# A top-32 attention with a metaformer block on one core: the next unit's halves are formed ahead of a unit's last maximum

## The chip, the cores and the metric

The kernel runs on one core of a Trainium2 chip. A core has five engines, each with a queue that is worked off in order: TensorE (PE in the profile; its weight loads are PEld), VectorE (DVE), ScalarE (ACT), GpSimd (POOL) and SyncE (SP, which here issues nearly all DMAs). Engines wait for each other by semaphores. The metric is the time of one execution on the device in microseconds; lower is better.

## The reference

For 8 batches, 8 heads, 576 rows and 64 columns a head, each row of scaled scores is cut to its 32 largest, softmax is taken over these, and the result is multiplied with the values. The heads are joined to rows of 512, and a layer norm, two matrix products with a ReLU between (512 to 2048 and back) and a residual follow.

```python
scores = scale * np.matmul(q, k.transpose(0, 1, 3, 2))
kth = np.partition(scores, -top_k, axis=-1)[..., -top_k:-top_k + 1]
scores = np.where(scores >= kth, scores, -1000000000.0)
scores = scores - np.max(scores, axis=-1, keepdims=True)
attn = np.exp(scores)
attn = attn / (np.sum(attn, axis=-1, keepdims=True) + 1e-09)
x = np.matmul(attn, v)            # heads joined to rows of 512
xn = (x - mu) / np.sqrt(var + 1e-06) * g_ln
out = x + np.maximum(xn @ w_ch1, 0.0) @ w_ch2
```

## The kernel before, in words

**Units.** A unit is 128 query rows of two heads, two tiles of 128 x 576 scores, or, for the 64 rows that 576 leaves over, one tile that holds these rows of both heads. There are 160 units, 128 of two tiles and 32 of one. A loop over n (in `compute`) takes one unit after the other, and in each round every engine gets work of several units: TensorE makes the scores of unit n + 2 (`scores`, line 438), VectorE selects in unit n, ScalarE and GpSimd mask unit n - 1, and the exponentials of unit n - 1 and n - 2 are turned and multiplied with the values.

**Selection on VectorE.** `halve` (line 447) forms the elementwise larger and smaller halves of a score row: line 461 writes 288 larger values to `hi`, line 462 the smaller to `lo`. `hi` has two homes, taken in turn by units, `lo` one. `select(u, i)` (line 464) finds eight maxima at a time (line 483) and strikes them out (line 469), for i from 0 to 3, so 32 in all; at i = 1 the eight largest of `lo` are added to the candidates (line 475). At i = 3 nothing is struck out: its eighth maximum is the unit's threshold `thr`.

**From the threshold on.** In the next round `prepare` lets ScalarE scale the threshold and the top (lines 495 and 496); `mask` makes a steep ReLU on ScalarE (line 532) and subtracts the scores on GpSimd (line 535). `watch` (line 502) notes on GpSimd whether a row had more than eight of its 32 among the smaller halves. `weigh` takes the exponential on ScalarE (line 543).

**Turning.** Attention weights are transposed in one of two ways: by TensorE (`turn`, line 606, evacuated by ScalarE, line 618), or, for most later units, "moved": VectorE transposes blocks of 32 (`move`, line 577), and two DMAs of SyncE carry them by way of memory into `pt` (lines 594 and 587). `values` (lines 669 and 677) multiplies them, ScalarE evacuates to `oT` (line 687), TensorE turns that (line 714), and ScalarE scales it into rows (line 691).

**Row work.** Finished rows get statistics on VectorE (`stats`, lines 742 and 743) and are centred on GpSimd (lines 748 and 751); TensorE turns them (line 778), ScalarE evacuates (line 781), and the products of lines 819 and 979 follow, whose ReLU (line 842) and sums are on ScalarE and GpSimd. In the first rounds the weights are converted too (lines 164 to 185, on ScalarE, GpSimd and, line 177, VectorE).

**Order.** The schedule is written out by hand (`manual_schedule`): instructions stand in each queue as the program issues them. Only the matrix products of the row work are placed by a planner: `fill` issues as many of them as a share per slot allows, from costs that are constants in the source. PSUM has 5 banks for short-lived tiles (scores, turned tiles, values) and 3 for the row work's products. Score tiles in SBUF have 5 buffers.

Of the kernel before, what the change touches and what calls it, by code (L numbers as in the profile page):

```python
# [29 lines left out]
def compute(  # L30
# [207 lines left out]
    def pop():  # L238
        kind, cost, run, may = todo.pop(0)
        assert not may or may()  # L240
        owed[0] -= cost
        run()
# [30 lines left out]
    def fill(least=0):  # L273
        tick[0] += 1
        loads.settle(LOAD_AGE)
        sends.settle(SEND_AGE)
        ends_later.settle(END_AGE)
        fetch_forms(FETCH_AGE)
        owed[0] = min(owed[0] + share[0], 6.0)
        while todo and (not todo[0][3] or todo[0][3]()):  # L280
            if owed[0] < todo[0][1] / 2 and least <= 0:
                break
            least -= 1
            pop()
# [162 lines left out]
    def halve(u):  # L447

        nt = len(u.tiles)
        u.lo = lopool.tile([P, 2, HALF], FP32, tag="lo", name="lo")
        u.hi = hi_homes[u.i % 2]
        sides = int(doubt is not None)
        u.low, u.body = (sides * LOWS + HALF, sides * LOWS) if doubt is None or u.i // 2 % 2 else (0, LOWS)
        a, b = u.sc[:, 0:nt, 0:HALF], u.sc[:, 0:nt, HALF:S]
        lo, hi = u.lo[:, 0:nt], u.hi[:, 0:nt, u.body : u.body + HALF]  # L460
        nc.vector.tensor_tensor(hi, a, b, ALU.max)  # L461
        nc.vector.tensor_tensor(lo, a, b, ALU.min)  # L462

    def select(u, i):

        nt = range(len(u.tiles))

        def replace(m, t, x):
            nc.vector.match_replace(x, m[:, t, :], x, LOWEST)  # L469

        if i == 1:
            for r in range(low_rounds):
                o = u.low + 8 * r
                for t in nt:
                    nc.vector.max(u.hi[:, t, o : o + 8], u.lo[:, t])  # L475
                if r < low_rounds - 1:
                    for t in nt:
                        replace(u.hi[:, :, o : o + 8], t, u.lo[:, t])
        r0, width = (min(u.low, u.body), HALF + LOWS) if i > 1 else (u.body, HALF)
        pl = brief_small if i in (1, 2) else small  # L480
        m = pl.tile([P, 2, 8], FP32, tag=f"m{i}", name=f"m{i}")
        for t in nt:
            nc.vector.max(m[:, t, :], u.hi[:, t, r0 : r0 + width])  # L483
        if i < TOP_K // 8 - 1:
            for t in nt:
                replace(m, t, u.hi[:, t, r0 : r0 + width])
        if i == 0:
            u.top = m
        u.thr = m
# [47 lines left out]
    def weigh(u, t):  # L537
        g = u.group
        if g.den is None:
            g.den = denpool.tile([P, 2 * J + 1], FP32, tag="den", name="den")  # L540
        col = 2 * u.qt + t
        u.weighed += 1
        nc.scalar.activation(  # L543
            u.e[:, t], u.e[:, t], AF.Exp, bias=u.bias[:, t : t + 1], scale=-scale,
            accum_out=g.den[:, col : col + 1],
        )
        if u.rest:
            den = g.den[:, 2 * J : 2 * J + 1]
        elif u.weighed == 2 and u is [x for x in g.units if not x.rest][-1]:
            whole = [qt for qt in g.qts if qt < J]  # L550
            den = g.den[:, 2 * whole[0] : 2 * whole[-1] + 2]
            g.sums = den
        else:
            return
        nc.scalar.activation(den, den, AF.Copy, bias=DEN_EPS)
# [500 lines left out]
    def fetch_forms(age):  # L1056
        if done(formed[0]):
            free = 4 + sum(tick[0] - x >= age for x in used)
            while fetched[0] < min(free, 8 * (len(blocks) - PLAIN)):
                fetch_form()  # L1060
# [96 lines left out]
    def at(i):  # L1157
        return units[i] if 0 <= i < N else None
# [104 lines left out]
    for n in range(END):  # L1263
# [8 lines left out]
        u, nxt, mk = at(n), at(n + 1), at(n - 1)  # L1272
# [119 lines left out]
        if mk and len(mk.tiles) > 1 and mk.i >= EARLY:  # L1392
            weigh(mk, 1)
        fill()
        if u:
            select(u, 3)
        if nxt:
            halve(nxt)
        if n == 0:
            for x in batches[-1]:  # L1400
                x.shift()
# [27 lines left out]
@with_exitstack  # L1429
def kernel(  # L1430
    ctx: ExitStack,
    tc: tile.TileContext,
    *operands: bass.AP,
):
    nc = tc.nc
    doubt = ctx.enter_context(tc.tile_pool(name="doubt", bufs=1)).tile(
        [1, 1], I32, tag="doubt", name="doubt"
    )
    compute(tc, *operands, low_rounds=1, doubt=doubt[:])
    again = nc.values_load(  # L1440
        doubt[:], min_val=0, max_val=1,
        skip_runtime_bounds_check_because="a comparison's result",
    )
    with tc.If(again > 0):
        compute(tc, *operands, low_rounds=2, doubt=None)
# [31 lines left out]
```

## Time and profile before

| | before |
|---|---|
| median of 3 runs (lowest to highest) | 1571.86 us (1570.28 to 1573.63) |
| the profiled execution's own time | 1571.11 us |
| its span | 1569.2 us |
| busy: TensorE, VectorE | 1469.0 us (94%), 1363.4 us (87%) |
| busy: ScalarE, GpSimd | 1083.8 us (69%), 981.2 us (63%) |

A span runs from the first to the last instruction of the program in the profile. A group of instructions is shown by its line, engine and operation, what it writes and reads, its count, its busy time and mean, and the idle time of its engine just before it with what ended that. A row of the timeline has start, duration, engine, line and operation, and in brackets the idle time before it and what released it. A row of waits has the total in us, the number of waits and the longest. TensorE's instruction ends are modelled, so its busy share tells that it has work, not that it is at its peak.

### The profile page before, as it was taken

How to read it: one execution, taken by the hardware profiler on the slowest of the kernel's cores; microseconds unless marked ns; L12 is line 12 of the kernel's file. 1: busy time of each engine (PE TensorE's matmuls, PEld its weight loads, DVE VectorE, ACT ScalarE, POOL GpSimd, SP SyncE). 2: the span in 40 equal slices, each digit the busy share in tenths (PEclk: the TensorE clock that was granted, in tenths of full speed). 3: DMA queues.
4: the chain of work that ended last, by engine and by line, in shares of the span. 5: the costliest groups of instructions: out<-in, count | busy, mean ns of one | idle time of the engine just before them, and what ended most of it. 6: DMA issues, size and time to landing. Idle time of an engine off the chain costs nothing. (4 is left out here: it accounts for less than half of the span.)

```text
span 1569.2 us, 27215 instructions
## 1 busy us (share of the span) xinstructions
PE 1469.0 (94%) x8046; PEld 1108.0 (71%) x8046; DVE 1363.4 (87%) x3873; ACT 1083.8 (69%) x3081; POOL 981.2 (63%) x1318
## 2 busy tenths in 40 slices
PE   4568889999999999999999999999999998999997
PEld 3346446566787677778777777777777776788886
DVE  7997999899979998999988999999999999768000
ACT  6978887786777767767768676768676776555421
POOL 6968995747465565756566647474746475737524
PEclk9779989999999999999999999999999999999999
DMA  6623551466728865577754687657677557454511
GB/s 170 167 85 97 137 139 53 124 178 181 226 83 194 202 208 153 168 199 153 216 148 134 174 200 197 173 150 191 175 201 206 162 164 208 121 166 125 150 35 50
DMA packets 374774, 245.60 MB, mean 157 GB/s; under 512 B 255956, under 2 KB 343512, under 8 KB 374616
## 3 DMA queue, kind: packets, MB, share of 16 engines
q1 hardware_dynamic: 371048, 243.17, 57.6%
q8 instruction: 67, 1.10, 0.3%
q10 hardware_dynamic: 3568, 0.59, 0.3%
q14 instruction: 91, 0.75, 0.2%
HBM read 166.14 MB, written 77.53 MB: 155 GB/s over the span
## 5 line engine op out<-in xcount | busy, mean ns | idle before, releaser
L535 POOL TENSOR_TENSOR e<-e,sc 128x576 f32<-128x576 f32 x288 | 416.0, 1462 | 453.8 <-ACT e L532 392.9
L819 PE MATMUL hps<-xT,w 128*128 128x256 f32 x2304 | 542.2, 384 | 2.4 <-ACT xT L781 2.4
L819 PEld LDWEIGHTS hps<-xT,w 128*128 128x128 f32 x2304 | 423.0, 191 | 82.2 <-issue 27.2
L483 DVE MAX8 m<-hi 128x8 f32<-128x296 f32 (+1 forms) x1152 | 471.3, 444 | 1.2
L469 DVE MATCH_REPLACE8 hi<-m,hi 128x288 f32<-128x288 f32 (+1 forms) x864 | 377.0, 441 | 0.0
L979 PE MATMUL ops<-w,h 128*128 128x256 f32 x1280 | 304.8, 383 | 1.4 <-ACT o L944 1.4
L979 PEld LDWEIGHTS ops<-w,h 128*128 128x128 f32 x1280 | 233.6, 190 | 44.3 <-issue 13.5
L419 ACT COPY sc<-scps 128x288 f32<-128x288 f32 x576 | 188.5, 402 | 78.5 <-POOL e L535 56.2
L543 ACT ACTIVATE e<-e,m 128x576 f32<-128x576 f32 x288 | 225.1, 784 | 14.6 <-POOL e L535 12.5
L532 ACT ACTIVATE e<-sc,m 128x576 f32<-128x576 f32 x288 | 209.4, 769 | 0.0
L842 ACT ACTIVATE h<-hps 128x512 f32<-128x512 f32 x144 | 86.7, 602 | 114.1 <-PE hps L819 113.5
L577 DVE STREAM_TRANSPOSE sc<-e 128x1152 f32<-128x1152 f32 x87 | 118.8, 1366 | 52.5 <-ACT e L543 46.3
L669 PE MATMUL av<-pt,vb 128*64 128x256 f32 (+2 forms) x1280 | 148.8, 376 | 9.5 <-DMA pt<-turned 7.7
L462 DVE TENSOR_TENSOR lo<-sc 128x576 f32<-128x576 f32 (+1 forms) x160 | 136.1, 850 | 0.0
L461 DVE TENSOR_TENSOR hi<-sc 128x576 f32<-128x576 f32 (+1 forms) x160 | 130.0, 812 | 3.0 <-ACT sc L419 3.0
L669 PEld LDWEIGHTS av<-pt,vb 128*64 128x64 f32 x1280 | 81.6, 140 | 66.4 <-issue 17.1
L438 PE MATMUL scps<-kT,late_qT 64*128 64x288 f32 (+3 forms) x832 | 121.7, 410 | 0.2 <-ACT pt L618 0.2
L979 PE MATMUL ops<-wt,s 128*128 128x256 f32 x512 | 119.4, 383 | 0.0
L475 DVE MAX8 hi<-lo 128x8 f32<-128x288 f32 x288 | 117.5, 443 | 0.0
L438 PE MATMUL scps<-kT,qT 64*128 64x288 f32 x512 | 92.6, 460 | 23.5 <-DVE qT L366 8.0
L606 PE MATMUL tp<-ident,e 128*128 128x128 f32 x456 | 74.2, 290 | 39.9 <-ACT e L543 28.9
L979 PEld LDWEIGHTS ops<-wt,s 128*128 128x128 f32 x512 | 94.7, 190 | 17.3 <-issue 4.4
(111 smaller groups left out, 1793.5 us busy)
## 6 DMA issues: line engine op xcount, KB each, us to landing
turned<-sc SPq DMA_DIRECT2D x87, 576.0 KB, 4.2
pt<-turned SPq DMA_DIRECT2D x348, 144.0 KB, 3.2
w<-forms SPq DMA_DIRECT2D x128, 256.0 KB, 4.7
vb<-in_v_dram SPq DMA_DIRECT2D x80, 288.0 KB, 4.2
raw<-in_moe_w_ch_dram SPq DMA_DIRECT2D x32, 512.0 KB, 4.5
kT<-kept SPq DMA_DIRECT2D x48, 288.0 KB, 3.7
kept<-kT SPq DMA_DIRECT2D x32, 288.0 KB, 3.6
kqin<-in_k_dram SPq DMA_DIRECT2D x116, 72.0 KB, 2.6
```

Source lines behind the costliest of these rows:

```text
L419: nc.scalar.copy(u.sc[:, t, s * HALF : (s + 1) * HALF], u.made[s][t][:, 0:HALF])
L438: nc.tensor.matmul(ps[i * R : i * R + ql, o : o + width], qT[r, q0 : q0 + ql], kT[r, k0 : k0 + width], start=True, stop=True,)
L461: nc.vector.tensor_tensor(hi, a, b, ALU.max)
L462: nc.vector.tensor_tensor(lo, a, b, ALU.min)
L469: nc.vector.match_replace(x, m[:, t, :], x, LOWEST)
L483: nc.vector.max(m[:, t, :], u.hi[:, t, r0 : r0 + width])
L532: nc.scalar.activation(u.e[:, t], u.sc[:, t], AF.Relu, bias=u.edge[:, t : t + 1], scale=-STEEP)
L535: nc.gpsimd.tensor_tensor(u.e[:, t], u.e[:, t], u.sc[:, t], ALU.subtract)
L543: nc.scalar.activation(u.e[:, t], u.e[:, t], AF.Exp, bias=u.bias[:, t : t + 1], scale=-scale, accum_out=g.den[:, col : col + 1],)
L669: nc.tensor.matmul(av[h * D : (h + 1) * D, 0 : g.nq], vb[:, h * (J + 1) + c, :], heads_of(g, h, 0, g.nq // 32)[:, :, c], start=(c == 0), s ...
L819: nc.tensor.matmul(ps[0][:, side * N : (side + 1) * N], w1[:, c, f * P : (f + 1) * P], self.xT[:, c, 0:N], start=(c == 0), stop=(c == NC - 1),
L979: nc.tensor.matmul(bank[name][:, 0:Q], a(j), rhs, start=first and j == 0, stop=(j == G - 1), skip_group_check=not first,)
```

## The change

In each round the halves of the next unit are formed ahead of `select(u, 3)`, the last maxima of the present unit, instead of behind it. For a unit of two tiles VectorE's queue held, at the end of a round: two replacements of i = 2 (line 469), two maxima (line 483), one operation of line 461 and one of line 462. It now holds the two replacements, lines 461 and 462, and then the two maxima. What stands in the other engines' queues, and what each instruction waits for, is the same as before.

```diff
@@ -1392,10 +1392,10 @@
         if mk and len(mk.tiles) > 1 and mk.i >= EARLY:
             weigh(mk, 1)
         fill()
+        if nxt:
+            halve(nxt)
         if u:
             select(u, 3)
-        if nxt:
-            halve(nxt)
         if n == 0:
             for x in batches[-1]:
                 x.shift()
```

## The prediction

> **What bounds the kernel now.** I read the page's busy times, then busy time by stage, then the waits of ScalarE and TensorE stage by stage, and last the timeline of single units. One execution was profiled at 1571.11 us (span 1569.2 us and 1.9 us around it); the median of the three runs is 0.75 us higher.
>
> ```profile
> span 1569.2 us, 27215 instructions
> ...
> PE 1469.0 (94%) x8046; PEld 1108.0 (71%) x8046; DVE 1363.4 (87%) x3873; ACT 1083.8 (69%) x3081; POOL 981.2 (63%) x1318
> ```
>
> Busy time by stage (stretch, its length, then PE, PEld, DVE, ACT, POOL):
>
> ```profile
> 0.00:220.00 220.00, 154.48 (x721) 99.86 (x722) 194.51 (x524) 182.17 (x469) 178.90 (x171) 0.87 0.51 134
> ...
> 310.00:416.00 106.00, 102.89 (x554) 73.74 (x553) 105.79 (x312) 75.55 (x215) 62.44 (x85) 0.98 0.70 186
> ...
> 475.00:590.00 115.00, 109.02 (x607) 83.61 (x605) 114.86 (x333) 78.67 (x227) 66.20 (x93) 0.99 0.78 203
> ...
> 862.00:1316.00 454.00, 445.25 (x2430) 335.21 (x2428) 451.73 (x1303) 325.34 (x956) 276.15 (x411) 1.00 0.68 181
> 1316.00:1460.00 144.00, 143.21 (x739) 117.32 (x740) 104.89 (x284) 77.13 (x211) 84.53 (x122) 1.00 0.55 154
> ```
>
> TensorE is the bound of the whole: after 220 us it is idle for a few us per stage, and its instructions do not change, so the time moves only as its idle time moves. But the pacemaker alternates. In 310 to 416, 475 to 590 and 862 to 1316 VectorE is busy for over 99% and TensorE loses 3.1, 6.0 and 8.75 us; from 1316 on TensorE paces and VectorE has spare time.
>
> The threshold (the last maximum of a unit, line 483) reaches ScalarE at line 495. That wait over the whole run, and then in 220 to 310, 310 to 416, 475 to 590, 740 to 789 and 862 to 1316:
>
> ```profile
> ACT m L495 <- DVE m L483: 84.2, 51, 3.7
> ...
> ACT m L495 <- DVE m L483: 2.9, 1, 2.9
> ...
> ACT m L495 <- DVE m L483: 17.2, 8, 3.5
> ...
> ACT m L495 <- DVE m L483: 21.4, 10, 3.7
> ...
> ACT m L495 <- DVE m L483: 4.8, 4, 2.2
> ...
> ACT m L495 <- DVE m L483: 37.9, 28, 3.4
> ```
>
> The five stretches hold all 51 waits and 84.2 us. Elsewhere, in the first 220 us too, ScalarE comes later than the threshold. What TensorE waited for (stretch 220 to 310, then 310 to 416, 475 to 590, and from 1316 on):
>
> ```profile
> PE scps L438 <- ACT x L691: 2.4, 1, 2.4
> ...
> PE av L669 <- DMA pt<-turned: 2.3, 1, 2.3
> PE xo L714 <- ACT oT L687: 0.8, 1, 0.8
> ...
> PE tp L606 <- ACT sc L419: 1.6, 1, 1.6
> ...
> PE tp L778 <- ACT sc L419: 1.9, 1, 1.9
> ```
>
> So where VectorE paces, TensorE meets ScalarE's copies, which stand behind the wait for the threshold.
>
> **The change, part by part.** No instruction is added or removed; the two halvings of the next unit (lines 461 and 462) go in front of the last maxima. The other queues, SP's and POOL's too, keep their order and no DMA is moved. A plain unit of two tiles now, in the timeline:
>
> ```profile
> 1183.56 0.74 DVE L461 TENSOR_TENSOR hi<-sc 128x576 f32<-128x576 f32 x1
> 1183.68 0.21 ACT L495 ACTIVATE m<-m 128x2 f32<-128x2 f32 x1 [0.58 <-DVE m L483]
> ...
> 1184.21 0.75 DVE L462 TENSOR_TENSOR lo<-sc 128x576 f32<-128x576 f32 x1
> 1184.77 2.84 POOL L535 TENSOR_TENSOR e<-e,sc 128x576 f32<-128x576 f32 x2 [1.83 <-ACT e L532]
> 1184.88 0.81 DVE L483 MAX8 m<-hi 128x8 f32<-128x288 f32 x2
> ```
>
> (1) *The threshold's delay.* From the first halving to the next maximum is 1184.88 - 1183.56 = 1.32 us; that is how much later each threshold comes (about half where the next unit has one tile). Queued on ScalarE behind line 495 are line 496, the masks of line 532, the copies of line 419 and then everything that frees PSUM or feeds TensorE; POOL's subtraction waits for the masks. VectorE gains nothing by having the halves earlier: it reads them itself, one maximum later.
>
> (2) *Units with row statistics.* These put two statistics on VectorE and two centrings on POOL (line 751) just ahead of the last maxima:
>
> ```profile
> 955.79 0.69 POOL L751 TENSOR_SCALAR x<-x,less 128x512 f32<-128x512 f32 x1
> ...
> 956.13 0.81 DVE L483 MAX8 m<-hi 128x8 f32<-128x296 f32 x2
> ...
> 956.74 1.32 POOL L751 TENSOR_SCALAR x<-x,less 128x512 f32<-128x512 f32 x1
> 956.85 0.74 DVE L461 TENSOR_TENSOR hi<-sc 128x576 f32<-128x576 f32 x1
> ...
> 957.50 1.16 DVE L462 TENSOR_TENSOR lo<-sc 128x576 f32<-128x576 f32 x1
> ...
> 958.55 1.27 ACT L419 COPY sc<-scps 128x288 f32<-128x288 f32 x4
> ...
> 958.98 0.66 PE L606 MATMUL tp<-ident,e 128*128 128x128 f32 x4 [1.40 <-ACT sc L419]
> ```
>
> A halving and a POOL operation exclude each other here: the second centring takes 1.32 instead of 0.69 us while line 461 runs, and line 462 then 1.16 instead of 0.75. After the change line 461 would start at 956.13, still under the first centring (to 956.48, 0.35 us lost), and the second centring would still come between the halvings (some 0.6 us). That is 0.95 us of collision instead of 0.41, so about 0.5 us more VectorE time in each such unit, and a threshold late by 1.32 + 0.95 = 2.3 us. The Trainium skill (SBUF — State Buffer, Who interferes with whom) says that a VectorE instruction with two SBUF inputs and a GpSimd instruction that reads SBUF lock each other out for a whole instruction, whoever issues first. By that rule the collision moves rather than vanishes; the trace agrees, with 1.16 against 0.75 us.
>
> (3) *Units of one tile.* Their last maximum directly follows the replacement that it reads, and VectorE pauses; with two tiles another instruction lies between:
>
> ```profile
> 793.04 0.45 DVE L469 MATCH_REPLACE8 hi<-m,hi 128x296 f32<-128x296 f32 x1
> ...
> 793.52 0.47 DVE L483 MAX8 m<-hi 128x8 f32<-128x296 f32 x1
> ...
> 782.24 0.44 DVE L469 MATCH_REPLACE8 hi<-m,hi 128x296 f32<-128x296 f32 x1
> 782.60 0.82 DVE L483 MAX8 m<-hi 128x8 f32<-128x296 f32 x2
> ```
>
> 0.48 against 0.36 us from start to start: the halvings would fill that pause, 0.12 us for each of these units, 14 of which lie in 862 to 1316 (the count of the one-tile form, quoted below), 1.7 us. The Trainium skill (VectorE: DVE Perf Modes, The DRAIN you can't avoid) says that an operation's pipeline flush is paid whether or not a semaphore follows. Read strictly, this saving would be nothing and a sum that counts it 1.7 us higher; these rows speak for a saving.
>
> (4) *VectorE's own balance.* Some six statistics units lie in VectorE-paced stretches beside the two counted below: 6 x 0.5 = +3 us against -1.7 us. I take 0 and keep both ends for the range.
>
> (5) *What reaches TensorE.* Where VectorE paces, a constant delay does not add up from unit to unit: ScalarE and TensorE run 1.3 us later against VectorE, once. But when the stretch ends and TensorE paces, it starts that much later, and nothing there gives it back. So each stretch is charged once, by what TensorE met last in it. 220 to 310: a wait for ScalarE, 1.3 us. 310 to 416: the wait for ScalarE is followed by one of 2.3 us for a DMA whose source VectorE sends at an unchanged place, which swallows the first delay; after it only slack, so half, 0.7 us. 475 to 590: the last wait, 1.6 us, is in a statistics unit, 2.3 us. 740 to 789: no wait within, half, 0.7 us. 862 to 1316: the wait of 1.9 us at its end is behind a statistics unit again, 2.3 us. Sum: 1.3 + 0.7 + 2.3 + 0.7 + 2.3 = 7.3 us, which only a gain in (4) could cancel. In the first 220 us ScalarE is late by itself and hides the delay; if that cover went, 1.3 us more.
>
> 1571.1 + 7.3 = 1578.4 us; I predict 1578, 0.4% above the median.
>
> **The rivals.** *The delay is swallowed.* Against 51 late thresholds TensorE has some 20 short waits after 220 us, and DMA waits that do not move take up part of it. If only one of the two statistics ends reaches it, 1571.1 + 2.3 = 1573.4 us: no difference that can be told, since 0.2% (3.1 us) is about what a measurement of this kernel can tell from no change.
>
> *Faster, by fewer collisions.* The halvings now follow the threshold, and so run while ScalarE's masks wake POOL's subtraction; moved forward they might miss POOL. VectorE's groups in 862 to 1316 by form (count, busy us and mean ns, idle before):
>
> ```profile
> L577 DVE STREAM_TRANSPOSE sc<-e 128x1152 f32<-128x1152 f32 x38 | 51.9, 1365 | 0.0
> ...
> L462 DVE TENSOR_TENSOR lo<-sc 128x576 f32<-128x576 f32 x42 | 34.6, 825 | 0.0
> L461 DVE TENSOR_TENSOR hi<-sc 128x576 f32<-128x576 f32 x42 | 32.5, 775 | 0.0
> ...
> L462 DVE TENSOR_TENSOR lo<-sc 128x288 f32<-128x288 f32 x14 | 7.4, 526 | 0.0
> ```
>
> Against the undisturbed 0.74 and 0.75 us the 42 pairs of two tiles lose 42 x (0.035 + 0.075) = 4.6 us, and against 0.45 us the 14 of one tile 14 x 0.076 = 1.1: 5.7 us are collisions. If all went, with the 1.7 us of (3), VectorE would save 7.4 us there, less than TensorE's idle 8.75: 1571.1 - 7.4 = 1563.7 us, and 1571.0 with the handed-over 7.3. It decides from about 10 us saved, so it needs the first 220 us as well. Against it: in the plain unit the halvings are already undisturbed (0.74, 0.75).
>
> *Much slower, by the moved units.* VectorE's transposes (line 577) wait for the exponential, whose chain starts at the threshold. A tight place:
>
> ```profile
> 1070.95 0.19 ACT L543 ACTIVATION_READ_ACCUMULATOR e<-e,m 128x1 f32 x1
> ...
> 1073.11 1.37 DVE L577 STREAM_TRANSPOSE sc<-e 128x1152 f32<-128x1152 f32 x1
> ```
>
> The spare time is 1073.11 - 1071.14 = 1.97 us, over 1.32 but under 2.3. From 1.97 us on VectorE, the pacemaker, stalls. If TensorE's lateness doubles the delay (2.64 us), each such move costs up to 0.67 us; ten of them give 1578.4 + 6.7 = 1585 us.
>
> **How the numbers follow.** The forecast case, 1575 to 1582, 0.45; the moved units 0.13; swallowed 0.22; fewer collisions 0.20. So slower 0.58, same 0.22, faster 0.20. Low is 1567, between the two prices of the faster rival; high is 1588, the 1585 of the moved units with the +3 us of (4).
>
> **What would show it.** Right: line 495's wait on the threshold grows from 84 us in 51 waits to some 150 us, by about 1.3 us each; TensorE's waits for lines 419 and 687 grow by some 7 us in total and its other numbers stay; VectorE's pause in units of one tile is gone; line 751 stays long. Wrong: halvings with a clearly lower mean, VectorE's busy time down by 10 us or more, or line 577 waiting in 862 to 1316, where it now waits for nothing (0.0 in its row above).

## The result, and the profile after

The changed kernel takes 1584.05 us (median of 6 runs, 1583.22 to 1585.78), the kernel before on the same chip 1571.18 us (6 runs, 1569.75 to 1573.63). The ratio is 1.0082 (95% interval 1.0069 to 1.0095): 12.9 us slower. The forecast was 1578 us; the sign and the kind of loss came out, and the loss is nearly twice the 7.3 us that were forecast.

The page of the changed kernel (span, then busy time of the engines):

```profile
span 1582.5 us, 27215 instructions
...
PE 1469.8 (93%) x8046; PEld 1107.9 (70%) x8046; DVE 1372.3 (87%) x3873; ACT 1083.9 (68%) x3081; POOL 993.9 (63%) x1318
```

TensorE has as much work as before (1469.8 against 1469.0 us), so the loss is idle time of TensorE. VectorE is busy for 8.9 us more and GpSimd for 12.7, with the same instructions: they hold each other up more.

The waits of the changed kernel over the whole run (who waits for whom: total in us, number, longest):

```profile
ACT m L495 <- DVE m L483: 126.2, 67, 5.4
...
DVE sc L577 <- ACT e L543: 48.0, 12, 8.8
...
PE tp L606 <- ACT sc L419: 23.1, 14, 3.2
...
PE xo L714 <- ACT oT L687: 7.8, 10, 1.3
...
PE tp L778 <- ACT sc L419: 6.2, 2, 5.5
...
PE av L669 <- DMA pt<-turned: 3.2, 3, 1.7
```

Two of these rows in the kernel before:

```profile
PE tp L606 <- ACT sc L419: 10.9, 7, 2.1
...
PE av L669 <- DMA pt<-turned: 7.7, 6, 2.9
```

ScalarE waits for the threshold for 126.2 us instead of 84.2. The row of the value products' DMA had 7.7 us in 6 waits; it now has 3.2 in 3, which fits a ScalarE that is late and takes that time ahead of it. The waits for ScalarE's score copies (lines 606 and 778, both released by line 419) are 29.3 us where they were 14.5 (10.9 and 3.6).

Busy time by stage in the changed kernel (stretch, length, then PE, PEld, DVE, ACT, POOL, granted clock, DMA):

```profile
310.00:416.00 106.00, 100.83 (x545) 72.05 (x544) 105.79 (x309) 74.22 (x212) 61.26 (x83) 0.98 0.67 180
...
475.00:590.00 115.00, 105.74 (x589) 80.42 (x588) 114.90 (x336) 77.75 (x229) 65.29 (x93) 0.99 0.77 200
...
862.00:1316.00 454.00, 448.48 (x2427) 338.02 (x2426) 452.10 (x1290) 324.69 (x953) 285.82 (x413) 1.00 0.67 180
1316.00:1460.00 144.00, 137.99 (x711) 112.52 (x710) 115.04 (x306) 77.59 (x211) 87.37 (x125) 0.98 0.54 153
```

VectorE paces the same stretches as before, with over 99% busy. TensorE's idle time grows in 310 to 416 from 3.1 to 5.2 us, in 475 to 590 from 6.0 to 9.3, and in 1316 to 1460, which now begins with the end of the VectorE-paced stretch, from 0.8 to 6.0.

### The profile page after: what moved, and what is told of

It is laid out like the page before. It is cut to its first block, busy times and chain, and to the rows that moved or that the text cites. A ratio compares the mean times of both kernels' runs of the same rounds, so it can differ in the third digit from the quotient of the medians.

```text
span 1582.5 us, 27215 instructions
## 1 busy us (share of the span) xinstructions
PE 1469.8 (93%) x8046; PEld 1107.9 (70%) x8046; DVE 1372.3 (87%) x3873; ACT 1083.9 (68%) x3081; POOL 993.9 (63%) x1318
## 4 chain that ended last, share of the span: by engine, by line
PE 51%; DVE 30%; ACT 7%; DMA 4%; POOL 3%; SPq 2%; issue 1%; ACTq 0%; DVEq 0%; POOLq 0%
PE hps L819 20%; PE ops L979 16%; DVE m L483 9%; DVE hi L469 7%; PE scps L438 5%; PE av L669 5%; DVE sc L577 3%; DVE lo L462 3%; DVE hi L461 3%; DVE hi L475 2%; PE tp L606 2%; POOL e L535 1%; ACT e L532 1%; ACT e L543 1%; PE av L677 1%
## 5 line engine op out<-in xcount | busy, mean ns | idle before, releaser
L483 DVE MAX8 m<-hi 128x8 f32<-128x296 f32 (+1 forms) x1152 | 457.5, 442 | 0.3
L979 PE MATMUL ops<-w,h 128*128 128x256 f32 x1280 | 309.1, 387 | 1.0 <-ACT o L944 1.0
L669 PE MATMUL av<-pt,vb 128*64 128x256 f32 (+2 forms) x1280 | 144.2, 367 | 4.3 <-DMA pt<-turned 3.2
L462 DVE TENSOR_TENSOR lo<-sc 128x576 f32<-128x576 f32 (+1 forms) x160 | 144.1, 901 | 0.0
L461 DVE TENSOR_TENSOR hi<-sc 128x576 f32<-128x576 f32 (+1 forms) x160 | 133.2, 832 | 3.0 <-ACT sc L419 3.0
L495 ACT ACTIVATE m<-m 128x2 f32<-128x2 f32 (+1 forms) x160 | 33.2, 207 | 126.8 <-DVE m L483 126.2
L606 PEld LDWEIGHTS tp<-ident,e 128*128 128x128 f32 x456 | 58.8, 150 | 75.4 <-ACT e L543 32.3
```

What stands on the lines that cost most here:

```text
L669: nc.tensor.matmul(av[h * D : (h + 1) * D, 0 : g.nq], vb[:, h * (J + 1) + c, :], heads_of(g, h, 0, g.nq // 32)[:, :, c], start=(c == 0), s ...
L979: nc.tensor.matmul(bank[name][:, 0:Q], a(j), rhs, start=first and j == 0, stop=(j == G - 1), skip_group_check=not first,)
```

## The experiments

In what follows, the lag of TensorE is the start of a unit's first score product (line 438) in one trace minus its start in the trace of before; VectorE's lag is the same for a unit's first maxima. Both are worked out from the traces, one execution of each kernel, and executions differ: two of the kernels below issue the same instructions in the same order up to 365 us, and at 312 us their lags are -1.80 and -4.17 us. Each time stands beside runs of the kernel before on the same chip.

Three theories of the loss are held against each other. The *late-threshold theory* is that of the forecast: the threshold comes late to ScalarE, and at the end of a stretch that VectorE paces TensorE is left that much later. The *theory of VectorE's busy time* puts the loss down to the time that VectorE and GpSimd cost each other. The *theory of late exponentials* puts it down to VectorE's transposes (line 577) waiting for exponentials whose threshold was late.

**Only the larger half goes ahead.** Line 461 stands in front of the last maxima, line 462 stays behind them.

```diff
-        nc.vector.tensor_tensor(lo, a, b, ALU.min)
+        u.rest_of_halve = lambda: nc.vector.tensor_tensor(lo, a, b, ALU.min)
...
         if nxt:
             halve(nxt)
         if u:
             select(u, 3)
+        if nxt:
+            nxt.rest_of_halve()
```

> Only the larger half (line 461) goes ahead of the last maximum; the smaller half (line 462) stays behind it. The threshold then comes 0.74 us late in a plain unit of two tiles in place of 1.32. The late-threshold theory: each hand-over to TensorE at the end of a stretch paced by VectorE is about half as large, 0.7 us in place of 1.3 and 1.2 in place of 2.3, and waits of TensorE that stood at 3.0 and 3.2 us after the change stay near 2 us, so that fewer of them halve its clock: +3 to +7 us against the kernel before. The theory that VectorE's own additional busy time costs (collisions with GpSimd): it is line 462 that grew, from 0.92 to 0.99 us, and it is back at its old place, so 0 to +3 us. The theory of late exponentials (line 577): 0.74 us lies well under the spare time of 1.97 us, so about 0.

Measured: 1571.35 us against 1571.29, ratio 1.0005 (0.9995 to 1.0014): no loss. This answer is the one expected of the busy-time theory and of the late exponentials, and a miss for the late-threshold theory, which had +3 to +7. But the page and the first two stages of this kernel show that VectorE's busy time does not explain it either:

```profile
PE 1467.8 (94%) x8046; PEld 1107.5 (71%) x8046; DVE 1352.3 (86%) x3873; ACT 1084.4 (69%) x3081; POOL 989.2 (63%) x1318
```

```profile
0.00:220.00 220.00, 155.34 (x735) 99.83 (x736) 187.89 (x535) 184.79 (x476) 181.62 (x172) 0.84 0.52 137
220.00:310.00 90.00, 84.62 (x409) 54.54 (x409) 83.09 (x239) 68.00 (x186) 63.70 (x60) 0.96 0.29 85
```

VectorE is busy for 11.1 us less than before (1352.3 against 1363.4), 6.6 of them in the first 220 us (187.89 against 194.51), and the time is the same. TensorE is 1.8 us early at 312 us and 0.1 us late at the end. In this execution a saving met a loss of about its size at the ends of stretches, where TensorE still waits 2.1, 2.3 and 4.3 us in place of 1.6, 1.4 and 1.9 (near 562, 960 and 1316 us).

**Without the statistics rounds, and only there.** In one kernel the new order stands everywhere but in rounds with row statistics, in the other only in them.

```diff
+        with_stats = n in rows_of
...
-        if nxt:
-            halve(nxt)
-        if u:
-            select(u, 3)
+        if not with_stats:        # the other kernel: if with_stats
+            if nxt:
+                halve(nxt)
+            if u:
+                select(u, 3)
+        else:
+            if u:
+                select(u, 3)
+            if nxt:
+                halve(nxt)
```

> The new order everywhere except in the rounds that hold row statistics, which keep the old order. The late-threshold theory: the ends at 562, 960 and 1316 us are behind statistics units, so their waits go back to at most 1.9 us, the clock does not halve there, and of the 13 us +3 to +6 are left. The theory of VectorE's busy time: the plain units are most of the units, but the additional collisions are with the centrings, which exist only in the statistics rounds, so VectorE's busy time goes back by most of its 9 us and about +1 to +4 is left. This run does not tell these two apart by its time alone, but by VectorE's busy time beside it. The theory of late exponentials: those are spread over all units, so +8 to +12.

> The new order only in the rounds that hold row statistics, the old order in all others. The late-threshold theory: the waits at 562, 960 and 1316 us are there as after the change, with the halved clock behind them (1.3 to 3.6 us of wait and 1.7 to 3.4 us of half clock each): +6 to +10 us. The theory of VectorE's busy time: the collisions with the centrings are all there, +7 to +10 us, with VectorE's busy time up by nearly 9 us. The theory of late exponentials: +1 to +3.

Measured: without them 1580.22 us against 1571.29, ratio 1.0055 (1.0042 to 1.0068), +8.9; only in them 1577.23, ratio 1.0038 (1.0025 to 1.0051), +5.9. VectorE was busy for 1380.6 and 1367.1 us, 17.2 and 3.7 more than before. So most of the additional collisions are not, as I had expected, with the centrings: they are in the other rounds. The first time is a miss for both main theories (+3 to +6 and +1 to +4) and lies in the range of the late exponentials (+8 to +12), whose wait is not there, though: line 577 waits for 42.8 us in all, 46.3 before, and for nothing in 862 to 1316. The second lies just under the late-threshold theory's +6 to +10. And the time does not follow VectorE's busy time: +17.2 us of it go with 8.9, +3.7 with 5.9. That statistics rounds cost out of proportion because the ends of stretches lie behind them is what the next two runs test.

**Everywhere but at the ends, and only at the ends.** The ends are the 26 rounds in which the VectorE-paced stretches end.

```diff
-        if nxt:
-            halve(nxt)
-        if u:
-            select(u, 3)
+        # the other kernel: without "not"
+        if not any(a <= n <= b for a, b in ((34, 39), (54, 59), (79, 84), (142, 149))):
+            if nxt:
+                halve(nxt)
+            if u:
+                select(u, 3)
+        else:
+            if u:
+                select(u, 3)
+            if nxt:
+                halve(nxt)
```

> The new order everywhere except in 26 of 159 rounds, those in which the stretches paced by VectorE end (34 to 39, 54 to 59, 79 to 84 and 142 to 149). The late-threshold theory: what TensorE meets last in each stretch is as before the change, so the ends at 562 and 1316 us fall back to waits under 2 us with no halved clock; what is left is what is handed over within the stretches (416 and 970 us): +2 to +6 us. The theory of VectorE's busy time: 133 of 159 rounds keep their additional collisions, VectorE stays up by some 7 us, and +9 to +12 us are left. The theory of late exponentials: +9 to +12.

> The complement of the run before it: the new order only in the 26 rounds in which the stretches paced by VectorE end, the old order in the other 133. The late-threshold theory: TensorE meets late thresholds where it has no slack left, so most of the 13 us come back, less the part that 133 rounds alone had cost (2.8 us): +6 to +10 us, with waits of about 3 us near 562 us and over 4 us near 1320 us, and a halved clock behind them. The theory of VectorE's own busy time: 26 of 159 rounds, so VectorE's busy time is up by under 3 us and so is the time, 0 to +3. The theory of late exponentials: 0 to +2.

Measured: everywhere but at the ends 1574.13 us against 1571.29, ratio 1.0024 (1.0014 to 1.0034), +2.8 from 133 rounds; only at the ends 1578.67 against 1571.36, ratio 1.0051 (1.0038 to 1.0065), +7.3 from 26 rounds. The pages of the two, in this order:

```profile
PE 1465.6 (93%) x8046; PEld 1106.4 (70%) x8046; DVE 1372.3 (87%) x3873; ACT 1082.6 (69%) x3081; POOL 990.3 (63%) x1318
```

```profile
PE 1472.1 (93%) x8046; PEld 1110.1 (70%) x8046; DVE 1363.0 (86%) x3873; ACT 1084.9 (69%) x3081; POOL 980.9 (62%) x1318
```

The first has all of the changed kernel's additional VectorE time (1372.3) and a fifth of its loss; the second has none of it (1363.0 against 1363.4) and more than half of the loss. Both times are as the late-threshold theory expected (+2 to +6 and +6 to +10) and far from the other two (+9 to +12, then +3 or less). Most of the loss goes by where the threshold is late and not by how much VectorE does in all; what VectorE's additional time costs beside that is seen in the table by stretches below.

**The mirror image: an earlier threshold.** The row statistics of a round go behind the last maxima, once in the order of before and once in the changed one.

```diff
-        for blk, i in rows_of.pop(n, []):
-            blk.stats(i)
+        late_stats = rows_of.pop(n, [])
...
         if u:
             select(u, 3)
+        for blk, i in late_stats:
+            blk.stats(i)
```

> The order of before, but a round's row statistics (VectorE's two statistics and GpSimd's two centrings, lines 742 to 751) go from in front of the last maxima to behind them, ahead of the halvings. In those rounds the threshold comes earlier by the two statistics, about 1.5 us, and the centrings fall on the halvings and the next maxima. The late-threshold theory: the mirror image of the change. The waits at 562 and 1316 us (1.6 and 1.9 us) are behind such rounds and shrink to near nothing: -2 to -5 us against the kernel before. The theory of VectorE's busy time: as many instructions, and collisions of the halvings with the centrings as before or more: 0 to +3.

> The changed order (halvings in front of the last maxima everywhere) with the row statistics behind the last maxima. In the statistics rounds the threshold then is early by two statistics and late by two halvings, about where it was before the change, and the halvings no longer meet the centrings; all other rounds are as in the changed kernel. The late-threshold theory: the waits at 562, 970 and 1325 us fall back to at most 2 us and no clock is halved behind them; what is left is about what the new order outside of the statistics rounds had cost or less: +3 to +8 us against the kernel before, so 5 to 10 under the changed kernel. The theory of VectorE's busy time: it follows whatever VectorE's busy time does in this run, +9 us if that stays as in the changed kernel.

Measured: 1589.57 us against 1571.36, ratio 1.0118 (1.0103 to 1.0134), and with the changed order 1597.28, ratio 1.0163 (1.0149 to 1.0177). Both are far outside of what any theory gave. In the first kernel, TensorE's lag is still only 0.4 us at 1330 us of the kernel before, and the time goes lost after that. The first product of the last row block but one (line 778), in the timeline of before and then of this kernel:

```profile
1439.84 1.04 PE L778 MATMUL tp<-ident,x 128*128 128x128 f32 x8
```

```profile
1451.28 1.04 PE L778 MATMUL tp<-ident,x 128*128 128x128 f32 x8
```

The planner counts a block's age from its statistics; they came a slot later, and it put the last blocks' products elsewhere: TensorE's instructions differ from the order of before in 249 of 8046 places, all but 6 of them behind 1300 us. So this did not test the threshold. The second kernel loses some 16 us behind 1424 us of the kernel before, as the first does; it was not run again with the old plan. The first run was made again with the planner told the old time; TensorE's queue then has the order of before:

```diff
-        late_stats = rows_of.pop(n, [])
+        late_stats = [(blk, i, tick[0]) for blk, i in rows_of.pop(n, [])]
...
-        for blk, i in late_stats:
-            blk.stats(i)
+        for blk, i, when in late_stats:
+            blk.stats(i)
+            blk.step[i] = when
```

> As the run with the row statistics behind the last maxima, but the planner is told the time at which they stood before, so that the order of TensorE's queue is that of the kernel before. The statement to be tested is that the 18 us lost there came from the planner's later placing of the last blocks, not from the earlier threshold. The late-threshold theory with this: -1 to -5 us against the kernel before, since the waits of 1.6, 1.4 and 1.9 us at 562, 959 and 1316 us are behind such rounds and the threshold there comes about 1.6 us earlier. If an earlier threshold gains nothing, because the next wait at the same ends (for transposed weights, 1.4 us at 558 and 3.0 us at 1315 in that run) takes its place: -1 to +1. If the planner was not the cause: still +10 or more.

Measured: 1569.38 us against 1570.50, ratio 0.9995 (0.9986 to 1.0004). The 18 us were the planner's. And an earlier threshold (1.59 us in the statistics units of two tiles) gains nothing that can be told: TensorE's waits of 1.6 and 1.4 us at 562 and 959 us are gone, but one of 1.8 us for the value products stands at 556, and the last end's, 1.9 us for line 778, is as long as before. The median fits both answers, a small gain (-1 to -5) and none (-1 to +1). The profiled execution is ahead of before by 3.57 us, but it is the fastest of the eleven. So that a late threshold costs is shown; that an early one does not pay is not.

**The larger half ahead, but not at the ends.** The first experiment's kernel with the order of before in the 26 rounds:

```diff
-        if nxt:
-            halve(nxt)
-        if u:
-            select(u, 3)
+        if any(a <= n <= b for a, b in ((34, 39), (54, 59), (79, 84), (142, 149))):
+            if u:
+                select(u, 3)
+            if nxt:
+                halve(nxt)
+        else:
+            if nxt:
+                halve(nxt)
+            if u:
+                select(u, 3)
         if nxt:
             nxt.rest_of_halve()
```

> Only the larger half ahead of the last maxima, and in the 26 rounds at the ends of the VectorE-paced stretches the order of before. With the larger half alone VectorE was busy for 11 us less and the time was that of before. The late-threshold theory: that saving was spent at the ends, where 0.74 us of delay was still handed over (waits of 2.1, 2.3 and 4.3 us against 1.6, 1.4 and 1.9); with the old order there it shows: -1 to -4 us against the kernel before. The theory that the saving lies beside the path everywhere: 0.

Measured: 1569.83 us against 1571.36, ratio 0.9991 (0.9982 to 1.0000). A gain of 1.5 us, at the edge of what can be told, within what the late-threshold theory expected. No kernel tried here beats the one before by more.

**The halved clock.** After four of TensorE's waits the changed kernel's granted clock is 0.50: from 389.7, 567.2 and 970.0 us for 3.41 us each, and from 1325.0 us for 6.83. In the kernel before this happens twice, at 385.1 and 521.6. Windows of the changed kernel (columns as above; the granted clock is the third number from the end), at 389 and at 567 us:

```profile
386.30:389.70 3.40, 1.39 (x8) 0.91 (x7) 3.40 (x12) 2.23 (x7) 2.09 (x2) 1.00 0.12 37
389.70:393.10 3.40, 3.40 (x12) 2.73 (x11) 3.40 (x14) 3.01 (x10) 3.08 (x6) 0.50 0.99 253
563.80:567.20 3.40, 1.36 (x9) 1.26 (x10) 3.40 (x13) 3.37 (x10) 3.32 (x5) 1.00 1.00 241
567.20:570.60 3.40, 3.40 (x12) 2.65 (x11) 3.40 (x11) 2.49 (x10) 3.40 (x8) 0.50 1.04 347
```

In 3.4 us TensorE is idle for 2.0, and in the next 3.4 it runs at half speed, which loses 1.7 us of work. To take this away, unread matmuls were put into the idle time right behind (`BEHIND`) or ahead of (`AHEAD`) the value products of single groups, which these two tables name by their number (here those of the changed kernel):

```diff
+    groups_taken = [0]
+    AHEAD, BEHIND = {}, {16: 3, 28: 4, 56: 4, 72: 8}
+
+    def keep_busy(ps, count):
+        for _ in range(count):
+            nc.tensor.matmul(
+                ps[:, 256:512], ident[:], w1[:, 0, 0:256], start=True, stop=True
+            )
...
         av = brief("av")
+        keep_busy(av, AHEAD.get(groups_taken[0], 0))
...
+        keep_busy(av, BEHIND.get(groups_taken[0], 0))
+        groups_taken[0] += 1
         g.av = av
```

> The changed kernel, with matmuls that nobody reads (128x256 each, about 0.52 us, into unused columns of PSUM) right behind the value products of four groups: 3, 4, 4 and 8 of them, in the idle time ahead of TensorE's waits of 2.01, 2.98, 3.20 and 5.51 us at 389, 566, 970 and 1328 us of the changed kernel. They fill idle time only, so the late score copies come no earlier, but TensorE is no longer idle for 2 us in one stretch of 3.41 us. The theory that the granted clock of 0.5 behind those waits is part of the loss: no halved clock there, and 1.7 us less for each 3.41 us at half clock where TensorE paces behind it (567, and twice from 1325 on), less or nothing at 390 and 970 where VectorE paces: 3 to 7 us under the changed kernel, +6 to +10 us against the kernel before. The theory that the waits alone are the loss and the clock only shadows them: as the changed kernel, +13 us.

> The kernel before, with 3 and 4 such unread matmuls ahead of the value products of the two groups whose DMA waits of 2.33 and 2.94 us (at 384 and 522 us) the halved clock follows in that kernel. The clock theory: no halved clock at 385 and 522, where it lasted 3.41 us and cost 1.7 us each; VectorE paces both stretches, so TensorE's 1.7 us may be given back before they end: -3.4 to 0 us against the kernel before. If the clock plays no part: 0 to +1.

> The kernel with only the larger half ahead of the last maxima and the order of before at the ends of the VectorE-paced stretches, with 3 unread matmuls ahead of the value products near 381 us (wait of 1.98 us, then half clock) and 4 behind those near 952 us (wait of 2.69 us, then half clock). The clock theory: no halved clock in either place; both lie in stretches that VectorE paces, so 0 to 3.4 us less than without them, -1.5 to -5 us against the kernel before. If the clock plays no part: -1.5 as without them.

Measured: in the changed kernel 1582.17 us against 1571.07, ratio 1.0073 (1.0059 to 1.0086); in the kernel before 1571.87, ratio 1.0008 (0.9999 to 1.0017); in the kernel with the larger half ahead 1570.12, ratio 0.9997 (0.9988 to 1.0006). In the changed kernel the clock did stay up behind the first three places. Behind the fourth it is halved for one window in place of two (from 1328.6 us), and a new one stands at 523.0, behind a wait of 1.77 us for a DMA; an unread matmul took 0.38 us, less than the 0.52 expected. Two of the same windows with the unread matmuls:

```profile
389.70:393.10 3.40, 3.40 (x21) 3.04 (x22) 3.40 (x14) 3.38 (x13) 3.23 (x6) 1.00 1.03 267
...
567.20:570.60 3.40, 3.40 (x20) 2.69 (x20) 3.40 (x9) 2.93 (x11) 3.40 (x7) 1.00 0.53 176
```

21 and 20 records instead of 12 and 12 in the same 3.4 us. TensorE's lag against the changed kernel falls by 1.25 us behind the first place and by another 1.1 behind the second; at 970 us the 1.7 us are given back within 30 us, where VectorE paces. But at 1293 us, still ahead of the last end, VectorE loses the same amount by a collision (VectorE, GpSimd):

```profile
1293.40 1.16 DVE L461 TENSOR_TENSOR hi<-sc 128x576 f32<-128x576 f32 x1
1294.49 1.96 DVE L462 TENSOR_TENSOR lo<-sc 128x576 f32<-128x576 f32 x1
```

```profile
1292.54 3.29 POOL L535 TENSOR_TENSOR e<-e,sc 128x576 f32<-128x576 f32 x2 [7.81 <-ACT e L532]
1295.80 0.71 POOL L502 TENSOR_TENSOR watched<-hi,m 128x2 f32<-128x2 f32 x1
```

In the changed kernel the two halvings of this unit took 0.74 and 0.75 us. The time, 11.1 us over the kernel before, lies between the two answers (+6 to +10 and +13), so this run is a miss for the clock as a main cause: the medians with and without the matmuls differ by 1.9 us and their intervals overlap. How much the collision took from the other executions is not known: the profiled one, 1584.16 us, is one of the two slowest of five. In the kernel before with unread matmuls the clock halves at 958 and 1316 us instead, behind waits of 2.8 and 2.5 us. The third kernel has no halved clock from 300 us to its last 6 us, and is no faster than it was with two. The halved clock is a loss that can be seen locally; that it reaches the time is not shown in any of the three.

**Not settled.** In the first 54 us the kernels with the new order outside of statistics rounds bring TensorE forward by 1.6 to 2.0 us. The traces show where it comes from, though no run tests it: a GpSimd conversion (line 171) takes 3.01 us from 18.85 us in the kernel before, where VectorE runs line 461, line 462 and three conversions (line 177) without a break, and 1.47 us from 18.73 us in the changed kernel, where the last maximum stands between them. GpSimd's subtraction (line 535) then starts at 28.74 in place of 30.34 us, and behind it TensorE's first transposes (line 606) at 31.35 in place of 33.21. The loss of the two complementary kernels is 14.8 us for statistics and other rounds, 10.1 for ends and other rounds, and 12.9 for the change: the parts do not add up. That what one end hands over changes which collisions follow is a likely reason, and not shown.

## Why the prediction was right or wrong, point by point

TensorE's lag gained in each stretch, in us, by the forecast's fifth step and as the traces have it (a stretch's value is taken where TensorE paces behind it; one execution of each kernel):

| stretch | forecast | changed kernel | only at the ends | all but the ends |
|---|---|---|---|---|
| up to 310 | 1.3 | -1.50 | 0.17 | -0.60 |
| 310 to 416 | 0.7 | 2.91 | 0.67 | -0.37 |
| 475 to 590 | 2.3 | 4.08 | 1.60 | 0.74 |
| 590 to 740 | 0 | 0.51 | 0.79 | 0.48 |
| 740 to 789 | 0.7 | 1.61 | 1.07 | 0.26 |
| 862 to 1316 | 2.3 | 5.44 | 3.26 | 3.12 |
| sum | 7.3 | 13.05 | 7.56 | 3.63 |

**Step 5, the hand-over: right in its mechanism, and in its sum partly by luck.** A late threshold is handed to TensorE once per VectorE-paced stretch, at its end, and is kept from there. The kernel that has only these late thresholds loses 7.56 us in the trace, and 7.3 by the medians, as forecast. Its parts agree less well: 1.60 and 3.26 us where 2.3 was forecast for each, next to nothing for the 1.3 up to 310 us, and 0.79 where none was forecast.

**Step 1, the threshold's delay: right.** In 72 units of two tiles without statistics, from 220 to 1316 us and with another unit of two tiles behind them, the threshold is late against the unit's first maxima by 1.33 us in the middle, where 1.32 were forecast.

**Step 2, the statistics units: wrong in both of its numbers.** The place of the kernel before that stood at 955.79 to 958.98, in the changed kernel's timeline:

```profile
964.75 0.69 POOL L751 TENSOR_SCALAR x<-x,less 128x512 f32<-128x512 f32 x1
...
965.08 0.97 DVE L461 TENSOR_TENSOR hi<-sc 128x576 f32<-128x576 f32 x1
965.41 0.69 POOL L748 TENSOR_SCALAR less<-mv 128x1 f32<-128x1 f32 x1
965.97 0.74 DVE L462 TENSOR_TENSOR lo<-sc 128x576 f32<-128x576 f32 x1
966.20 1.08 POOL L751 TENSOR_SCALAR x<-x,less 128x512 f32<-128x512 f32 x1
...
966.64 1.54 DVE L483 MAX8 m<-hi 128x8 f32<-128x296 f32 x4
...
969.51 0.70 PE L606 MATMUL tp<-ident,e 128*128 128x128 f32 x4 [3.20 <-ACT sc L419]
```

I had the second centring come between the halvings, at VectorE's cost. It is GpSimd that waits: its small line 748 takes 0.69 us (0.19 at 964.46), the centring starts only at 966.20 and takes 1.08, and line 462 runs undisturbed. VectorE loses 0.23 us, not 0.95 (before: 0.41), and the threshold is late by 1.56 us, not 2.3. That line 751 stays long is wrong too: its mean in 862 to 1316 falls from 892 to 764 ns.

**Step 3, the pause in units of one tile: right.** The row of line 483 in 862 to 1316 has no idle time left (0.0 us, 0.5 before), and in 27 such units without statistics the operation behind the replacement starts 0.368 us after it in the middle, where it was 0.485: a gain of 0.12 us, as forecast. Here the Trainium skill's rule that the flush is always paid (VectorE: DVE Perf Modes, The DRAIN you can't avoid), read strictly, would have given nothing; the same section adds that an operation that is not held starts earlier, and the saving that these rows show is measured.

**Step 4, VectorE's own balance: taken as 0, measured +2.4 us in 862 to 1316, and the term with the largest error.** VectorE's lag grows there from 8.6 to 10.9 us. Its groups of this stretch by form (columns: busy us, mean ns, idle before):

```profile
L483 DVE MAX8 m<-hi 128x8 f32<-128x296 f32 x192 | 79.4, 446 | 0.0
...
L577 DVE STREAM_TRANSPOSE sc<-e 128x1152 f32<-128x1152 f32 x38 | 51.9, 1365 | 0.0
...
L462 DVE TENSOR_TENSOR lo<-sc 128x576 f32<-128x576 f32 x41 | 34.8, 849 | 0.0
L461 DVE TENSOR_TENSOR hi<-sc 128x576 f32<-128x576 f32 x41 | 33.2, 811 | 0.0
...
L461 DVE TENSOR_TENSOR hi<-sc 128x288 f32<-128x288 f32 x14 | 8.9, 639 | 0.0
...
L462 DVE TENSOR_TENSOR lo<-sc 128x288 f32<-128x288 f32 x15 | 8.5, 569 | 0.0
```

Against the undisturbed 0.74, 0.75 and 0.45 us, collisions are 41 x (0.071 + 0.099) + 14 x 0.189 + 15 x 0.119 = 11.4 us, where the forecast counted 5.7 before. The stretch holds other units now, since all is later; over the same units of both kernels the collisions grow from 6.1 to 10.2 us, and the rounds with statistics have 2.0 in both. So the growth is not theirs. The plain unit that the prediction showed undisturbed, now:

```profile
1191.34 0.46 POOL L909 TENSOR_TENSOR s<-h 128x128 f32<-128x128 f32 x1
...
1191.54 0.88 DVE L461 TENSOR_TENSOR hi<-sc 128x576 f32<-128x576 f32 x1
1191.89 0.85 POOL L910 TENSOR_TENSOR s<-s,h 128x128 f32<-128x128 f32 x1
1192.35 1.00 DVE L462 TENSOR_TENSOR lo<-sc 128x576 f32<-128x576 f32 x1
1192.70 0.97 POOL L911 TENSOR_TENSOR h<-h 128x128 f32<-128x128 f32 x1
...
1193.27 1.54 DVE L483 MAX8 m<-hi 128x8 f32<-128x296 f32 x4
...
1194.13 0.21 ACT L495 ACTIVATE m<-m 128x2 f32<-128x2 f32 x1 [1.75 <-DVE m L483]
```

And before:

```profile
1181.34 0.47 POOL L909 TENSOR_TENSOR s<-h 128x128 f32<-128x128 f32 x1
...
1181.89 0.45 POOL L910 TENSOR_TENSOR s<-s,h 128x128 f32<-128x128 f32 x1
...
1182.31 0.46 POOL L911 TENSOR_TENSOR h<-h 128x128 f32<-128x128 f32 x1
...
1182.81 0.83 DVE L483 MAX8 m<-hi 128x8 f32<-128x296 f32 x2
1183.56 0.74 DVE L461 TENSOR_TENSOR hi<-sc 128x576 f32<-128x576 f32 x1
```

Lines 909 to 911 are GpSimd's sums of the row work. Before, they ran while VectorE struck out maxima, ahead of the halvings; now the halvings fall on them, and both engines get slower. Two moves bring this about. Against VectorE's other work the halvings come 0.75 us earlier, to 1182.81 us of the kernel before, where line 911 has just ended (1182.77). And GpSimd's work comes later: it stands behind ScalarE's masks, which wait for the late threshold, and in 862 to 1316 lines 909 to 911, 535 and 790 come 1.2 to 1.3 us later against VectorE in the middle. I had counted the threshold's delay for ScalarE and the subtraction in step 1, and left GpSimd's rows where they were in steps 2 and 4. I also weighed only the centrings and line 535, and the rule of step 2 (SBUF — State Buffer, Who interferes with whom, in the Trainium skill), which these rows bear out, should have been asked of all that GpSimd does in the 2 us ahead of the halvings in the trace of before. The kernel with the new order everywhere but at the ends has this term nearly by itself: VectorE's lag grows by 2.2 us in this stretch (0.9 to 3.1) and TensorE's by 3.12, the end's hand-over included.

**The sum.** In the changed kernel the 13.05 us can be split by VectorE's lag at the end of each stretch (-0.59, 2.27, 7.05 and 10.91 us at 413, 586, 790 and 1315 us of the kernel before) and TensorE's behind it (1.41, 5.49, 7.61 and 13.05). What VectorE's lag gains over TensorE's last value is step 4: 0.9, 0.9, 1.1 and 3.3, in all 6.1 us where I took 0. What TensorE's lag has over VectorE's is the hand-over: 2.0, 3.2, 0.6 and 2.1, in all 7.9 us where 0.7, 2.3, 0.7 and 2.3 make 6.0. Beside these, the 1.3 us up to 310 came out as a gain of 1.5, and 0.5 us came in from 590 to 740. So the forecast's mechanism holds, and the term that failed most is step 4. Of the kernels with a part of the change, 7.6 us at the ends and 3.6 beside them make 11.2 of the 13.05; the rest shows only with both together (2.6 us of it in 310 to 416). I had also given the hand-over of 310 to 416 as half hidden behind a DMA wait (0.7); with the new order everywhere it was not.

The measured 1584 us lies above the forecast case's own stretch, 1575 to 1582, and under the high end of 1588. That is partly luck: 1588 was made of the moved units, which did not come, and of the +3 us of step 4, which did.

**The rivals.** *Swallowed* fell with the result. *Fewer collisions* had the sign of the collisions wrong; only the first 310 us gained, 1.5 us. *Moved units* gave nearly the measured time (1585 us), but its mechanism is absent: line 577 waits for nothing in 862 to 1316 and for 48.0 us in all, 46.3 before. The threshold's waits grew to 126.2 us in 67 (150 forecast), and TensorE's for lines 419 and 687 by some 19 us where 7 were forecast: they are more than the whole loss, and TensorE's waits for DMA (line 669) and for line 691 shrank by 4.5 and 4.0 us beside them.

## What to carry to other kernels

Where two engines take turns as the pacemaker, price a delay at the end of each stretch, and what the pacing engine itself gains or loses within it, and test it there: 26 of 159 rounds held more than half of the loss, while 8.9 us more or 11.1 us less of VectorE's busy time moved the time by 2.8 and 0.1 us. When an instruction with two SBUF inputs is moved, list everything that GpSimd does at the new place, not only what it met at the old one, and shift GpSimd's own rows first by the delay that the move hands them (1.2 to 1.3 us here). When a step moves, look also at what a planner reads from its position: that alone cost 18 us.

## What was not expected of the hardware

TensorE's granted clock falls to 0.50 for a window of 3.41 us after pauses well under 3 us. The windows lie on a fixed grid (in the kernel before 385.1 and 521.6 us begin two of them, 40 windows apart), and it is the idle time within one window that counts. Pauses of 2.98 us at 566 us and of 3.22 us at 564 us, the second of the kernel with the new order only at the ends, cut by a window's edge into 1.4 and 1.8:

```profile
559.30:562.70 3.40, 1.96 (x12) 1.07 (x8) 3.37 (x8) 0.24 (x3) 3.03 (x5) 1.00 0.43 142
562.70:566.10 3.40, 1.62 (x10) 1.50 (x11) 3.40 (x14) 3.40 (x10) 3.37 (x4) 1.00 0.96 264
566.10:569.50 3.40, 3.40 (x21) 2.94 (x20) 3.40 (x9) 3.38 (x12) 3.40 (x8) 1.00 0.92 287
```

The longer pause leaves the clock at 1.00, the shorter one (row 563.80 above, 2.0 us idle in its window) halves it. After 300 us, over all 14 traces, every window with 1.95 us or more of idle time was followed by half clock, none at full clock with under 1.6 was, and between them both occurred. Waits of 2.3 us at 384 and 520 us in the kernel with the planner's old time were cut by window edges too (1.74 and 1.39 us in one window), and its clock stayed at 1.00. The Trainium skill (TensorE: Matmul & The Clock Gate, What's actually happening) describes a free-running window of 3413 ns and a half clock after one idle window; the window and the half are as these runs show, but 2.0 of its 3.4 us idle were enough here.
